# An attention and two mixtures in one kernel: the units of a head pair's round in another order, mask products as units of their own, the first mixture's early product in four pieces

## The chip, the cores and the metric

The kernel runs on one core of a Trainium2 chip. The metric is the time of one execution on the device in microseconds (us), as the median of repeated runs. The engines of the core work side by side, each in its own program order: TensorE (PE in the profile, its weight loads PEld), VectorE (DVE), ScalarE (ACT), GpSimd (POOL), and SyncE (SP), which here issues the DMAs. An engine waits for another by a semaphore, and then all that stands behind the waiting instruction on that engine waits too.

## The reference, cut to what matters

```python
def _attn_ref(q, k, v):                      # 4 batches, 8 heads, 576 tokens, 64 wide
    scores = scale * np.matmul(q, k.transpose(0, 1, 3, 2))
    scores = np.where(block_i >= block_j, scores, -1000000000.0)   # blocks of 64 tokens
    attn = np.exp(scores - np.max(scores, axis=-1, keepdims=True))
    attn = attn / (np.sum(attn, axis=-1, keepdims=True) + 1e-09)
    return np.matmul(attn, v)
...
def _moe_ref(x, w_in, w_out):                # x: 2304 x 512, w_in: 512 x 2048
    h = x @ w_in
    g = np.where(h >= 1, h, np.where(h <= -1, 0.0, (h + 1) ** 2 / 4))
    return g @ w_out
...
def _moe2_ref(x, phi, w1, w2):               # soft mixture: 8 experts, 4 slots each
    logits = x @ phi                         # softmax over tokens gives the slots' inputs,
    ...                                      # two products per expert, softmax over slots combines
```

The attention's output, turned to 2304 tokens by 512, is the first mixture's x, and that mixture's output is the second one's.

## The kernel before

The attention comes first and works on **pairs**: two heads of one batch, 16 pairs, one `Pair` object each. After it, `Moe.run` does the rest of the first mixture and the second. Only the attention's part of the program and a few early steps of the first mixture that are laid into it are touched.

What a pair needs is cut into small **units**, methods of `Pair` that each give one engine a few instructions. `lk`, `lq`, `lv` load keys, queries and values (SP). `kh`, `kl`, `qh`, `ql` split keys and queries into a high and a low part (ACT, POOL, ACT, DVE; `ql` also issues two small DMAs that lay out the last 64 queries, `QD`). `sc4` to `sc0` multiply scores (PE): three products of the parts; for `sc0` to `sc3` the two halves of a 64-row pair run on the two row halves of the array, and two small products with `low` and `one` then add the mask; `sc4` has no mask. `mx` takes the maxima (DVE), `ex` the exponentials with their sums (ACT), `rs` the reciprocal of the sums (DVE), `no` scales by it (POOL). `pt0` to `pt6` turn the scaled blocks, 25 of them, by products with the identity (PE), and `pc0` to `pc6` copy each group of up to four blocks out of PSUM (ACT, groups 1 and 3 DVE). `pa` and `pb` multiply by the values (PE) and `xh`, `xl` write the result out of PSUM as x (ACT and DVE, in high and low part for the first 1024 tokens, else one DVE copy). `w0`, `w1`, `w2` prepare a half of a 128-column strip of w_in (a load by SP; one ACT and four DVE instructions; three POOL ones, the last two of them sums of two arrays).

The order is written out by hand in the string `PLAN`. Each entry is a unit with a digit ahead of it; in round `it` it is done for pair `it - digit`. The entries' order is the program's order, in which each engine takes the units that are its own. Eleven **early units** of the first mixture (`EARLY`) go in from round 9 on, one a round: the entry `hm` is the product of one strip of w_in with 512 tokens (12 matmuls, each 512 columns, into one PSUM bank `h`), `ha` the first step of the bend (ACT) and `ho` the last two (DVE), after which the bank is free. The 64-row pair's scores have two PSUM tiles (`psc`), the values' product of `pa` has one (`ppv`), and all else, the groups `p0` to `p6`, the product `o` of `pb` and the early product `h`, takes turns in three banks (`ptr`): whoever takes a bank waits until its last content is copied out. The order in which the banks are given back in the program decides which one comes next.

From line 273 on, `attention` makes a list of (pair, unit) from `PLAN`, and calls the units one by one. The profile calls lines 120 and 123 the scores and their masks, 113 `sc4`, 166 the turning, 184 and 189 the values' product, 527 the early product, 142 and 140 the maxima, 147 the exponentials, 152 and 153 the reciprocal, 158 the scaling, 83 `kl`, 248 and 250 the copies, 545 `ha`, 558 and 559 `ho`.

Of the kernel before, what the change touches and what calls it, by code (L numbers as in the profile page):

```python
# [7 lines left out]
F32 = mybir.dt.float32  # L8
# [6 lines left out]
P = 128  # L15
# [21 lines left out]
class Pair:  # L37
# [69 lines left out]
    def sc(self, i):  # L107
        e, nc = self.e, self.nc
        sc = self.scs[i] = e.psc.tile([P, 2, 512], F32, tag="sc", name=f"sc{self.nm}{i}")
        if i == 4:  # L110
            for k, (qa, ka) in enumerate(((0, 0), (0, 1), (1, 0))):
                for u in range(2):
                    nc.tensor.matmul(sc[:, u, 0:288], self.QD[:, qa], self.K[:, ka, 288 * u:288 * u + 288],
                                     start=(k == 0), stop=(k == 2))
            return
        n = 128 * (i + 1)
        rows = slice(0, 64), slice(64, 128)
        for k, (qa, ka) in enumerate(((0, 0), (0, 1), (1, 0))):
            for h, r in enumerate(rows):
                nc.tensor.matmul(sc[:, h, 0:n], self.Q[r, qa, 128 * i:128 * i + 128], self.K[r, ka, 0:n],  # L120
                                 start=(k == 0), stop=False)
        for h, r in enumerate(rows):
            nc.tensor.matmul(sc[:, h, n - 64:n], e.low[r], e.one[r], start=False, stop=True)  # L123

    def block(self, i):
        for u, b in enumerate(self.TILES[i]):
# [18 lines left out]
    def ex(self, i):  # L145
        for b, sc, pr in self.block(i):
            self.nc.scalar.activation(pr, sc, AF.Exp, bias=self.negm[:, b:b + 1], accum_out=self.sums[:, b:b + 1])  # L147
# [66 lines left out]
    def xl(self, a):  # L214
        for hi, lo, src in self.xparts(a):
# [4 lines left out]


PLAN = """
3sc4 4pc2 4no1 1ho0 4pt4 3ex2 2qh 4pt5 4pc5 3sc1 4pc4 3rs0 3mx4 3mx1 5pa
3ex4 3ex1 2ql 5xh1 5pb 2w2 5xh0 3rs2 3no2 4pc3 3no3 5xl1 3sc0 2sc3
3pt0 3mx0 3no4 5xl0 3pt1 1kh 1lq 2mx3 3lv 3ex0 3rs1 3pc1 4pt6 2sc2 0hm0
2mx2 1w1 3pc0 4pc6 2ex3 0ha0 1kl 0lk 3pt2 3pt3 3no0 0w0
"""
EARLY = {(9, 0): (0, 0), (10, 0): (0, 1), (11, 0): (0, 2), (12, 0): (0, 3), (13, 0): (1, 0), (14, 0): (0, 4),
         (15, 0): (1, 1), (16, 0): (0, 5), (17, 0): (1, 2), (18, 0): (0, 6), (19, 0): (1, 3)}
# [12 lines left out]
def attention(e, tc, nb=4, wl=(1, 1 + 2 * READY)):  # L242
    nc = tc.nc
    e.ENG = ENG

    def copy(eng, dst, src):
        if eng == "A":
            nc.scalar.copy(dst, src)  # L248
        elif eng == "D":
            nc.vector.tensor_copy(dst, src)  # L250
        else:
            nc.gpsimd.tensor_scalar(out=dst, in0=src, scalar1=1.0, scalar2=1.0, op0=ALU.mult, op1=ALU.mult)
    e.copy = copy
    e.eng = lambda c: nc.vector if c == "D" else nc.gpsimd

    e.QD, e.pr, e.v_ = [], [], []
    for i in range(2):
        e.QD.append(e.apool.tile([P, 2, P], F32R, tag=f"QD{i}", bufs=1, name=f"QD{i}"))
        z = (nc.gpsimd, nc.vector)[i]
        z.memset(e.QD[i][0:64, :, 64:P].bitcast(F32), 0.0)  # L260
        z.memset(e.QD[i][64:P, :, 0:64].bitcast(F32), 0.0)
        e.pr.append([e.apool.tile([P, P * (b // 2 + 1)], F32, tag=f"pr{i}{b}", bufs=1, name=f"pr{i}{b}")
                     for b in range(9)])
        z.memset(e.pr[i][8][:, 576:640], 0.0)
        e.v_.append(e.apool.tile([P, 5, 2, 64], F32, tag=f"natv{i}", bufs=1, name=f"vn{i}"))
        z.memset(e.v_[i][64:P, 4], 0.0)
    e.low = e.apool.tile([P, P], mybir.dt.bfloat16, tag="low", bufs=1, name="low")
    e.one = e.apool.tile([P, 64], mybir.dt.bfloat16, tag="one", bufs=1, name="one")
    nc.vector.memset(e.low, 0.0)
    nc.vector.memset(e.one, 1.0)  # L270
    for h in (0, 64):
        nc.vector.memset(e.low[h:h + 1, 0:64], -2.0 ** 127)
    pairs = [Pair(e, nc, b, p) for b in range(nb) for p in range(4)]
    n = len(pairs)
    plan = [(it - int(u[0]), u[1:]) for it in range(n + 6) for u in PLAN.split()]
    plan = [(i, u) for i, u in plan if ((i, int(u[2:])) in EARLY if u[0] == "h" and u[1] in "moa" else
                                        0 <= i < n if u[0] != "w" else wl[0] <= i < wl[1])]
    fill = [(int(u[0]), u[1:]) for u in FILL.split()]
    assert sorted(fill) == sorted(plan[:len(fill)])
    for i, u in fill + plan[len(fill):]:  # L280
        if u[0] == "h":
            e.moe.early(u[1], *EARLY[i, int(u[2:])])
        elif u[0] != "w":
            pairs[i].step(u)
        else:
            t, c = (i - wl[0]) // 2, slice((i - wl[0]) % 2 * 256, (i - wl[0]) % 2 * 256 + 256)
            if u == "w0" and c.start == 0:
                e.moe.w_raw(t)
            elif u == "w1":
                e.moe.w_mul(t, c)  # L290
                e.moe.w_bits(t, c)
            elif u == "w2":
                e.moe.w_parts(t, c, e.ENG["w"])
# [14 lines left out]
class Moe:  # L308
# [207 lines left out]
            self.g[b, f] = self.new([P, a, n], F32, f"g{b}_{f}")  # L516
        return self.g[b, f // a * a][:, f % a]

    def h_unit(self, b, f, mid=()):
        e, nc = self.e, self.nc  # L520
        n = self.BLK[b][1]
        w = self.w[f].rearrange("p a (k c) -> p a k c", k=4)
        ph = self.ph[b, f] = e.ptr.tile([P, 512], F32, tag="tr", name=f"h{b}_{f}")
        m = 0
        for kk in range(4):
            for wi, xi in ((0, 0), (0, 1), (1, 0)):
                nc.tensor.matmul(ph[:, 0:n], w[:, wi, kk], self.x(b, kk, xi)[:, 0:n], start=(m == 0), stop=(m == 11))  # L527
                m += 1
            if kk == 2:
                for fn, *a in mid:  # L530
                    getattr(self, fn)(*a)
        if f == 15:
            self.drop_x(b)
        if b == 4:
            self.drop(f"w{f}")
# [23 lines left out]
        nc.vector.tensor_tensor(out=g, in0=ph, in1=g, op=ALU.max)  # L559

    def early(self, what, b, f):
        if what == "m":
            self.h_unit(b, f)
        elif what == "a":
            self.bend_act(b, f, "D")
        else:
            self.bend_max(b, f, "D")
# [547 lines left out]
def tile_attention_mixtures(ctx, tc, q, k, v, w_in, w_out, phi, w1, w2a, w2b, outa, outb):  # L1115
# [33 lines left out]
    with tc.tile_pool(name="att", bufs=1, reuse_waits="tile") as e.apool:  # L1149
        attention(e, tc)  # L1150
        nc.sync.dma_start(e.phi, phi.rearrange("(k p) s -> p k s", p=P))
# [53 lines left out]
```

## Time and profile before

| | |
|---|---|
| median of 3 runs | 538.68 us (538.38 to 539.71) |
| the profiled execution | 538.28 us, of which 536.5 us are the span from its first to its last instruction |
| busy share of the span | PE 95%, PEld 72%, DVE 64%, ACT 60%, POOL 38% |
| mean granted TensorE clock | 0.985 |
| first scores; first product of `Moe.run` | 5.6 us; 209 us |

A row of the trace's timeline has the start in us, the time in us from there to the last end of a group of equal instructions, the engine and line, the operation with its tiles (output, then inputs), the shape and the number of instructions. In brackets stands how long the engine sat idle just before, and what ended that. The starts of two groups give what the first of them cost its engine; a group's own time overlaps the next by the tail of the last product.

### The profile page before, as it was taken

The page shows a single profiled execution, that of the slowest core. Times are in us where ns is not written, and L with a number is a line of the kernel's source. Part 1 is how long each engine was busy: PE and PEld are TensorE (multiplying, and loading weights), DVE is VectorE, ACT ScalarE, POOL GpSimd, SP SyncE. Part 2 cuts the span into 40 slices and gives each one's busy share as a digit, 9 for nine tenths or more (in the row PEclk, how much of TensorE's full clock was granted, in tenths as well). Part 3 has the DMA queues.
Part 4 walks back from the last instruction along what each step waited for, and adds up shares of the span by engine and source line. Part 5 has one row for each costly group of instructions (what it writes and reads, how often), then busy time and mean ns, then how long its engine had stood idle before and what let it go on. Part 6 is the DMA issues. An engine that isn't in the chain of part 4 may idle for free.

```text
span 536.5 us, 11758 instructions
## 1 busy us (share of the span) xinstructions
PE 507.3 (95%) x4538; PEld 384.6 (72%) x4538; DVE 343.0 (64%) x676; ACT 322.4 (60%) x732; POOL 201.6 (38%) x259
## 2 busy tenths in 40 slices
PE   6899999999999989999989999899999999989994
PEld 5687777777777767878767887788767888643463
DVE  7799998888886734888998645823464343531242
ACT  5899987777777642667768878634334545231131
POOL 4888986767775430555552212500001000010000
PEclk9799999999999999999999999999999999999997
DMA  4444454323221135412146875322176496799997
GB/s 154 118 125 124 117 129 121 101 85 110 73 72 51 28 106 188 160 46 78 41 137 230 281 265 168 121 93 83 25 258 227 158 374 217 256 339 399 410 413 303
DMA packets 42711, 91.01 MB, mean 170 GB/s; under 512 B 8736, under 2 KB 18080, under 8 KB 42656
## 3 DMA queue, kind: packets, MB, share of 16 engines
q1 hardware_dynamic: 42656, 90.26, 49.6%
q8 instruction: 36, 0.59, 0.5%
q14 instruction: 19, 0.16, 0.1%
HBM read 74.51 MB, written 14.68 MB: 166 GB/s over the span
## 4 chain that ended last, share of the span: by engine, by line
PE 65%; DVE 14%; ACT 7%; DMA 5%; issue 3%; POOL 0%; SPq 0%; DVEq 0%; ACTq 0%; POOLq 0%
PE h L527 32%; PE gn L581 5%; PE om L184 4%; PE sc L120 4%; PE lt L593 3%; PE s L631 3%; PE eh L987 3%; DMA ew<-in_w2b_dram 3%; ACT pr L147 2%; DVE nm L142 2%; DVE wab L455 2%; DVE g L559 2%; DVE g L558 2%; ACT g L545 1%; PE om L189 1%
## 5 line engine op out<-in xcount | busy, mean ns | idle before, releaser
L527 PE MATMUL h<-xh,w 128*128 128x512 f32 (+1 forms) x384 | 115.6, 368 | 0.0
L158 POOL TENSOR_SCALAR pr<-pr,sm 128x384 f32<-128x384 f32 (+2 forms) x144 | 86.3, 617 | 38.4 <-DVE sm L153 14.0
L527 PE MATMUL h<-xt,w 128*128 128x512 f32 x384 | 91.6, 395 | 1.7 <-ACT PT L248 1.7
L558 DVE SCALAR_TENSOR_TENSOR g<-g 128x512 f32<-128x512 f32 (+1 forms) x52 | 37.4, 720 | 82.3 <-ACT g L545 81.7
L147 ACT ACTIVATE pr<-sc,nm 128x512 f32<-128x512 f32 (+2 forms) x144 | 78.6, 559 | 11.9 <-DVE nm L142 8.6
L527 PEld LDWEIGHTS h<-xt,w 128*128 128x128 f32 x384 | 70.5, 188 | 18.6 <-ACT PT L248 2.1
L527 PEld LDWEIGHTS h<-xh,w 128*128 128x128 f32 x384 | 69.1, 189 | 13.7 <-issue 3.8
L545 ACT ACTIVATE g<-h,half 128x512 f32<-128x512 f32 (+1 forms) x52 | 32.4, 623 | 62.5 <-PE h L527 62.0
L527 PE MATMUL h<-xl,w 128*128 128x512 f32 (+1 forms) x192 | 68.2, 355 | 0.2 <-POOL xl L400 0.2
L559 DVE TENSOR_TENSOR g<-h,g 128x512 f32<-128x512 f32 (+1 forms) x80 | 50.8, 636 | 16.0 <-ACT g L550 14.0
L142 DVE TENSOR_REDUCE nm<-sc 128x2 f32<-128x1024 f32 (+1 forms) x64 | 51.8, 818 | 5.0 <-PE sc L123 4.4
L662 POOL TENSOR_TENSOR cn<-cn,cm 128x128 f32<-128x128 f32 (+1 forms) x5 | 1.9, 378 | 140.7 <-DVE cm L661 111.2
L120 PE MATMUL sc<-K,Q 64*128 64x512 f32 (+3 forms) x384 | 47.0, 360 | 3.6 <-ACT pr L147 3.2
L248 ACT COPY gn<-gn 128x1024 f32<-128x1024 f32 x35 | 35.3, 1009 | 16.0 <-PE gn L581 15.8
L527 PEld LDWEIGHTS h<-xl,w 128*128 128x128 f32 x192 | 36.4, 189 | 4.5 <-POOL xl L400 0.7
L120 PEld LDWEIGHTS sc<-K,Q 64*128 64x128 f32 x384 | 29.9, 194 | 13.3 <-ACT pr L147 6.7
L472 POOL TENSOR_TENSOR wab<-wab,w 128x256 f32<-128x256 f32 (+1 forms) x23 | 22.5, 980 | 40.9 <-ACT w L248 20.4
L465 POOL TENSOR_TENSOR wab<-wab 128x512 f32<-128x512 f32 x16 | 21.9, 1372 | 40.4 <-DVE wab L457 27.3
L581 PE MATMUL gn<-ident,g 128*128 128x128 f32 x280 | 36.5, 273 | 0.2 <-ACT gn L248 0.2
L581 PEld LDWEIGHTS gn<-ident,g 128*128 128x128 f32 x280 | 31.9, 140 | 5.4 <-issue 2.5
L455 DVE SCALAR_TENSOR_TENSOR wab<-wab 128x512 uint32<-128x512 uint32 (+1 forms) x39 | 28.5, 731 | 9.8 <-ACT wab L448 6.9
L547 ACT ACTIVATE g<-h,half 128x512 f32<-128x512 f32 x28 | 19.3, 688 | 22.5 <-PE h L527 20.1
(221 smaller groups left out, 901.7 us busy)
## 6 DMA issues: line engine op xcount, KB each, us to landing
ew<-in_w_dram SPq DMA_DIRECT2D x32, 512.0 KB, 6.3
raw<-in_w_in_dram SPq DMA_DIRECT2D x16, 512.0 KB, 5.3
raw<-in_w_out_dram SPq DMA_DIRECT2D x16, 512.0 KB, 4.1
ew<-in_w2a_dram SPq DMA_DIRECT2D x16, 510.0 KB, 8.8
ew<-in_w2b_dram SPq DMA_DIRECT2D x16, 344.0 KB, 6.8
kn<-in_k_dram SPq DMA_DIRECT2D x16, 288.0 KB, 3.9
qn<-in_q_dram SPq DMA_DIRECT2D x16, 288.0 KB, 3.2
vn<-in_v_dram SPq DMA_DIRECT2D x16, 256.0 KB, 3.3
```

The costliest lines, as they stand in the source:

```text
L120: nc.tensor.matmul(sc[:, h, 0:n], self.Q[r, qa, 128 * i:128 * i + 128], self.K[r, ka, 0:n], start=(k == 0), stop=False)
L142: nc.vector.tensor_reduce(out=self.negm[:, 2 * i:2 * i + 2], in_=self.scs[i][:, :, 0:128 * (i + 1)], axis=AX.X, op=ALU.max, negate=True)
L147: self.nc.scalar.activation(pr, sc, AF.Exp, bias=self.negm[:, b:b + 1], accum_out=self.sums[:, b:b + 1])
L158: self.nc.gpsimd.tensor_scalar(out=pr, in0=pr, scalar1=self.sums[:, b:b + 1], scalar2=1.0, op0=ALU.mult, op1=ALU.mult)
L248: nc.scalar.copy(dst, src)
L455: v.scalar_tensor_tensor(out=Au, in0=Au, scalar=3, in1=Bu, op0=ALU.logical_shift_left, op1=ALU.bitwise_or)
L472: p.tensor_tensor(out=A, in0=A, in1=w[:, 0].bitcast(F32), op=ALU.subtract)
L527: nc.tensor.matmul(ph[:, 0:n], w[:, wi, kk], self.x(b, kk, xi)[:, 0:n], start=(m == 0), stop=(m == 11))
L545: nc.scalar.activation(g, ph, AF.Relu, bias=e.half[:, 0:1], scale=0.5)
L558: nc.vector.scalar_tensor_tensor(out=g, in0=g, scalar=1.0, in1=g, op0=ALU.min, op1=ALU.mult)
L559: nc.vector.tensor_tensor(out=g, in0=ph, in1=g, op=ALU.max)
L581: nc.tensor.transpose(ps[:, j, i * P:(i + 1) * P], self.gt(b, f)[:, o:o + P], e.ident)
```

## The change

Three things change. The mask's two products leave `sc` and are the unit `mk`, with entries of their own in the plan. The early product is cut into four units of three matmuls, `hm`, `hx`, `hy` and `hz`, by the four 128-row slices of x; the bank is taken at `hm`. And `PLAN` has all its entries in another order, with other digits: a round begins elsewhere, and some units are done a round later for their pair.

```diff
-        for h, r in enumerate(rows):
-            nc.tensor.matmul(sc[:, h, n - 64:n], e.low[r], e.one[r], start=False, stop=True)
+
+    def mk(self, i):
+        n = 128 * (i + 1)
+        for h, r in enumerate((slice(0, 64), slice(64, 128))):
+            self.nc.tensor.matmul(self.scs[i][:, h, n - 64:n], self.e.low[r], self.e.one[r], start=False, stop=True)
...
 PLAN = """
-3sc4 4pc2 4no1 1ho0 4pt4 3ex2 2qh 4pt5 4pc5 3sc1 4pc4 3rs0 3mx4 3mx1 5pa
...
+4pt1 4pc0 3mx3 4rs1 4no4 3sc2 4lv 3mk2 5pc6 4pc1 0w0 2kl 6xh1 5pt5 1hm0
+0lk 3mx2 4no1 4pt3 6xl1 3ex3 5pc5 4pt2 4pc3 3sc4 4no0 1hx0 3mx4 1hy0 2qh
...
-    plan = [(i, u) for i, u in plan if ((i, int(u[2:])) in EARLY if u[0] == "h" and u[1] in "moa" else
+    plan = [(i, u) for i, u in plan if ((i, int(u[2:])) in EARLY if u[0] == "h" and u[1] in "mxyzoa" else
...
+    def h_part(self, b, f, kk):
+        e, nc = self.e, self.nc
+        n = self.BLK[b][1]
+        if kk == 0:
+            self.ph[b, f] = e.ptr.tile([P, 512], F32, tag="tr", name=f"h{b}_{f}")
+        ph, w = self.ph[b, f], self.w[f].rearrange("p a (k c) -> p a k c", k=4)
+        for m, (wi, xi) in enumerate(((0, 0), (0, 1), (1, 0))):
+            nc.tensor.matmul(ph[:, 0:n], w[:, wi, kk], self.x(b, kk, xi)[:, 0:n], start=(kk + m == 0), stop=(kk + m == 5))
+
...
         for kk in range(4):
-            for wi, xi in ((0, 0), (0, 1), (1, 0)):
-                nc.tensor.matmul(ph[:, 0:n], w[:, wi, kk], self.x(b, kk, xi)[:, 0:n], start=(m == 0), stop=(m == 11))
-                m += 1
+            self.h_part(b, f, kk)
...
     def early(self, what, b, f):
-        if what == "m":
-            self.h_unit(b, f)
+        if what in "mxyz":
+            self.h_part(b, f, "mxyz".index(what))
```

On every engine the instructions are the same in number and kind; only their order differs. Names below: `h0_2` is the early product of batch of tokens 0 with strip 2, `ps2_0p2` group `p2` of batch 2, pair 0, `sc2_14` the scores `sc4` of batch 2, pair 1.

TensorE in a round with an early product, before: the twelve matmuls of `h` stand together, behind them `p2`, `p3`, `sc4` and then `p4` and `p5` of one pair.

```order
L527 MATMUL h0_2_1691<-xt00_140,w2_918 128x512 x3
L527 MATMUL h0_2_1691<-xt01_141,w2_918 128x512 x3
L527 MATMUL h0_2_1691<-xt02_142,w2_918 128x512 x3
L527 MATMUL h0_2_1691<-xt03_143,w2_918 128x512 x3
L166 MATMUL ps2_0p2_1719<-ident_116,pr08_176 128x128
...
L166 MATMUL ps2_0p3_1724<-ident_116,pr05_173 128x128
...
L113 MATMUL sc2_14_1733<-K_2_1_1482,QD1_180 128x288 x6
L166 MATMUL ps2_0p4_1745<-ident_116,pr00_168 128x128
...
L166 MATMUL ps2_0p5_1754<-ident_116,pr08_176 128x128
```

The same place now:

```order
L169 MATMUL ps1_3p5_1689<-ident_116,pr18_191 128x128
...
L530 MATMUL h0_2_1694<-xt00_140,w2_1040 128x512 x3
L169 MATMUL ps2_0p3_1703<-ident_116,pr05_173 128x128
...
L169 MATMUL ps2_0p2_1712<-ident_116,pr08_176 128x128
...
L113 MATMUL sc2_14_1718<-K_2_1_1460,QD1_180 128x288 x6
L530 MATMUL h0_2_1694<-xt01_141,w2_1040 128x512 x3
L530 MATMUL h0_2_1694<-xt02_142,w2_1040 128x512 x3
L530 MATMUL h0_2_1694<-xt03_143,w2_1040 128x512 x3
L169 MATMUL ps2_0p4_1744<-ident_116,pr00_168 128x128
...
L187 MATMUL ps1_3o_1750<-PT1_3_1481,vn1_193 64x256 x2
```

`p5` is now turned one round later and stands ahead of `h`; three of `h`'s matmuls come ahead of `p3`, `p2` and `sc4`, nine behind them, and the part `o` of the values' product follows `p4` ahead of `sc1`, where before it followed `pa`.

ScalarE at the same place, before: the bend of `h` (`g`) stands between the exponentials of `sc3` and the copy of `p2`.

```order
L147 ACTIVATE pr17_190,sm2_1_1670<-sc2_13_1643,nm2_1_1669 128x512
L545 ACTIVATE g0_2_1714<-h0_2_1691,half_129 128x512
L248 COPY PT2_0_1678<-ps2_0p2_1719 128x512
L147 ACTIVATE pr14_187,sm2_1_1670<-sc2_12_1682,nm2_1_1669 128x384
L147 ACTIVATE pr15_188,sm2_1_1670<-sc2_12_1682,nm2_1_1669 128x384
L89 ACTIVATE Q_2_2_1752<-qn2_2_1667 128x576
L248 COPY PT2_0_1678<-ps2_0p5_1754 128x512
```

And now:

```order
L150 ACTIVATE pr17_190,sm2_1_1668<-sc2_13_1634,nm2_1_1667 128x512
L252 COPY PT1_3_1481<-ps1_3p5_1689 128x512
L89 ACTIVATE Q_2_2_1734<-qn2_2_1392 128x576
L150 ACTIVATE pr14_187,sm2_1_1668<-sc2_12_1673,nm2_1_1667 128x384
L150 ACTIVATE pr15_188,sm2_1_1668<-sc2_12_1673,nm2_1_1667 128x384
L252 COPY PT2_0_1665<-ps2_0p2_1712 128x512
L150 ACTIVATE pr18_191,sm2_1_1668<-sc2_14_1718,nm2_1_1667 128x576
L551 ACTIVATE g0_2_1773<-h0_2_1694,half_129 128x512
```

The bend of `h` has moved behind the exponentials of `sc2` and `sc4`, and the copy of `p5`, whose bank `p2` takes, stands behind the exponentials of `sc3`.

## Rows read from the trace of the kernel before

**Rows 1.** Busy time by stretch: us, each engine's busy time, clock, DMA.

```profile
9.93:69.59 59.66, 55.64 (x546) 44.44 (x546) 53.88 (x116) 53.58 (x165) 51.66 (x77) 0.91 0.44 123
69.59:185.06 115.47, 112.65 (x1072) 89.61 (x1072) 92.84 (x202) 85.65 (x249) 78.86 (x115) 1.00 0.30 84
```

**Rows 2.** Timeline of TensorE: sc4 of the first pair and of the seventh.

```profile
9.93 1.03 PE L113 MATMUL sc<-K,QD 128*128 128x288 f32 x6 [2.66 <-DVE wab L456]
...
69.59 1.06 PE L113 MATMUL sc<-K,QD 128*128 128x288 f32 x6 [0.24 <-ACT pr L147]
```

**Rows 3.** Timeline of TensorE in one round with an early product.

```profile
133.29 1.03 PE L166 MATMUL ps_2p<-ident,pr 128*128 128x128 f32 x8
134.08 1.05 PE L113 MATMUL sc<-K,QD 128*128 128x288 f32 x6
134.97 1.37 PE L166 MATMUL ps_2p<-ident,pr 128*128 128x128 f32 x8
136.27 0.62 PE L120 MATMUL sc<-K,Q 64*128 64x256 f32 x6
136.74 0.21 PE L123 MATMUL sc<-one,low 64*128 64x64 bf16 x2
136.87 1.74 PE L184 MATMUL om<-PT,vn 128*64 128x256 f32 x16
...
139.77 0.55 PE L120 MATMUL sc<-K,Q 64*128 64x128 f32 x6
140.16 0.20 PE L123 MATMUL sc<-one,low 64*128 64x64 bf16 x2
140.20 0.94 PE L120 MATMUL sc<-K,Q 64*128 64x512 f32 x6
...
142.38 0.79 PE L120 MATMUL sc<-K,Q 64*128 64x384 f32 x6
...
143.18 3.06 PE L527 MATMUL h<-xt,w 128*128 128x512 f32 x12
146.08 1.03 PE L166 MATMUL ps_3p<-ident,pr 128*128 128x128 f32 x8
```

**Rows 4.** Timeline of TensorE: four turnings behind sc4, two rounds earlier.

```profile
110.38 0.66 PE L166 MATMUL ps_0p<-ident,pr 128*128 128x128 f32 x4 [0.70 <-DVE g L559]
```

**Rows 5.** Timelines of VectorE and ScalarE: one maximum, one exponential, one copy.

```profile
46.55 1.22 DVE L142 TENSOR_REDUCE nm<-sc 128x2 f32<-128x1024 f32 x1
...
117.07 0.58 ACT L248 COPY PT<-ps_1p 128x512 f32<-128x512 f32 x1
...
117.70 0.72 ACT L147 ACTIVATE pr<-sc,nm 128x512 f32<-128x512 f32 x1
```

**Rows 6.** Timeline of TensorE at the end of the attention.

```profile
185.06 1.04 PE L113 MATMUL sc<-K,QD 128*128 128x288 f32 x6
...
191.27 1.09 PE L166 MATMUL ps_3p<-ident,pr 128*128 128x128 f32 x8
...
193.83 3.02 PE L527 MATMUL h<-xt,w 128*128 128x512 f32 x12 [1.32 <-ACT PT L248]
...
209.09 4.15 PE L527 MATMUL h<-xt,w 128*128 128x512 f32 x17
```

**Rows 7.** Timelines of GpSimd (kl) and VectorE (reciprocals' first step), rounds without early product.

```profile
44.40 0.15 DVE L152 TENSOR_SCALAR sm<-sm 128x1 f32<-128x1 f32 x1
...
47.68 0.65 DVE L152 TENSOR_SCALAR sm<-sm 128x4 f32<-128x4 f32 x1
...
46.88 1.42 POOL L83 TENSOR_TENSOR K<-kn,K 128x576 fp32r<-128x576 f32 x1
```

**Rows 8.** Timeline of ScalarE at the start: second pair's keys, first strip's weights.

```profile
6.61 0.67 ACT L248 CAST K<-kn 128x576 fp32r<-128x576 f32 x1 [1.48 <-DMA kn<-in_k_dram]
...
8.06 0.43 ACT L448 ACTIVATE wab<-raw 128x256 f32<-128x256 f32 x1 [0.79 <-DMA raw<-in_w_in_dram]
```

**Rows 9.** Chain that ended last, near the end: start, us, what.

```profile
501.95 8.59 DMA ew<-in_w2b_dram
```

More of the change, by code (lines that the diff above doesn't have):

```diff
@@ L222 @@
 PLAN = """
-3sc4 4pc2 4no1 1ho0 4pt4 3ex2 2qh 4pt5 4pc5 3sc1 4pc4 3rs0 3mx4 3mx1 5pa
-3ex4 3ex1 2ql 5xh1 5pb 2w2 5xh0 3rs2 3no2 4pc3 3no3 5xl1 3sc0 2sc3
-3pt0 3mx0 3no4 5xl0 3pt1 1kh 1lq 2mx3 3lv 3ex0 3rs1 3pc1 4pt6 2sc2 0hm0
-2mx2 1w1 3pc0 4pc6 2ex3 0ha0 1kl 0lk 3pt2 3pt3 3no0 0w0
+4pt1 4pc0 3mx3 4rs1 4no4 3sc2 4lv 3mk2 5pc6 4pc1 0w0 2kl 6xh1 5pt5 1hm0
+0lk 3mx2 4no1 4pt3 6xl1 3ex3 5pc5 4pt2 4pc3 3sc4 4no0 1hx0 3mx4 1hy0 2qh
+2ql 3ex2 1hz0 4pt4 4pc2 5pb 3w2 0lq 3sc1 3ex4 3mk1 3rs0 1ha0 1ho0 5xh0
+4pc4 3no2 3mx1 5pa 2w1 3ex1 3sc0 3mk0 2sc3 5xl0 2mk3 1kh 3mx0 3rs2 3ex0
+4pt6 3no3 3pt0
 """
@@ L517, in gt, with h_unit @@
         return self.g[b, f // a * a][:, f % a]
-    def h_unit(self, b, f, mid=()):
+    def h_part(self, b, f, kk):
         e, nc = self.e, self.nc
         n = self.BLK[b][1]
-        w = self.w[f].rearrange("p a (k c) -> p a k c", k=4)
-        ph = self.ph[b, f] = e.ptr.tile([P, 512], F32, tag="tr", name=f"h{b}_{f}")
-        m = 0
+        if kk == 0:
[3 more added lines that the diff above has]
+            nc.tensor.matmul(ph[:, 0:n], w[:, wi, kk], self.x(b, kk, xi)[:, 0:n], start=(kk + m == 0), stop=(kk + m == 5))
+    def h_unit(self, b, f, mid=()):
         for kk in range(4):
-            for wi, xi in ((0, 0), (0, 1), (1, 0)):
-                nc.tensor.matmul(ph[:, 0:n], w[:, wi, kk], self.x(b, kk, xi)[:, 0:n], start=(m == 0), stop=(m == 11))
-                m += 1
+            self.h_part(b, f, kk)
             if kk == 2:
```

## The prediction

> **What bounds the kernel now.** I read the busy table of the page first, then the busy time by stretch, the chain of waits, and the timelines of the engines in single rounds. PE is busy 95% of the span, so nearly everything that a new order can give back is small waits of PE, and the change touches only the attention, the first 209 us. That part has three stretches. From `sc4` of the first pair to `sc4` of the seventh (9.93 to 69.59 us, [rows 2]) there are six rounds without an early product, 59.66 / 6 = 9.94 us each; VectorE, ScalarE and GpSimd are all busy for 52 to 54 of those 59.66 us, PE for 55.64 [rows 1]: nobody has room, and in the chain of waits the work of VectorE and ScalarE alternates. From there to `sc4` of the last pair come nine rounds with one, 115.47 / 9 = 12.83 us each; PE is busy 112.65 of 115.47 us, VectorE 92.84 [rows 1]: here PE is the bound. Then the pipeline drains, 185.06 to 209.09 us [rows 6].
>
> In a PE-bound round the question is what PE waits for. Eight turnings that follow `h` take 134.08 - 133.29 = 0.79 us; the eight behind `sc4` (`p4`, `p5`) take 136.27 - 134.97 = 1.30 us [rows 3]. The row that shows the reason stands two rounds earlier: the second four start late, and DVE L559 ended the wait [rows 4]. That is `ho`: `p5` takes the bank that `h` holds until the bend is done. So each round loses 0.51 us there, and more in the rounds where the row itself says 0.70.
>
> **The change part by part.** *Mask units.* `mk` stands on PE right behind its `sc` as before, since what was put between are units of SP, ACT and DVE. It costs and gives nothing; PE's order there is the same.
>
> *The round with an early product.* `p5` moves away from `h`'s bank: now it takes the bank that `p0`'s copy gives back, and the next user of `h`'s bank is `p0` of the next pair, at the round's end. The 0.51 us go. What is late next? `p2` now takes the bank of `p5`, whose copy on ACT stands behind the exponentials of `sc3`. Count from the start of `p1`: the masks of `sc3` ended some 0.5 us earlier (five turnings at 0.10). Its maximum takes 1.22, the two exponentials 2 x 0.72 less overlap, about 1.34, the copy 0.58 less overlap, about 0.5 [rows 5]: ready at about -0.5 + 1.15 + 1.35 + 0.5 = 2.5. PE reaches `p2` after `p1` 0.4, `sc2` with mask 143.18 - 142.38 = 0.8, `p5` 0.4, a quarter of `h` (146.08 - 143.18 = 2.90) 0.7 and `p3` 0.4, that is 2.7. The cover is thin, 0.2 us; if it goes, each tenth of a microsecond costs 9 x 0.1.
>
> The new order also splits groups. `pb` stands ahead of `sc1` and `pa` behind it, so the array changes its shape once more a round (64-row halves, full, 64-column halves: seven changes for six). A mask that is followed by the same shape costs 140.20 - 140.16 = 0.04 us, one that is followed by another shape 136.87 - 136.74 = 0.13 [rows 3]: +0.09 us. `p5` and `p4` stand alone now, each between 0 and 0.66 - 0.40 = 0.26 us dearer [rows 4]; PE does not wait there, so I take them at nothing. Sum: 12.83 - 0.51 + 0.09 = 12.4 us, bounds 12.2 (the rounds with the longer wait gain more) and 12.83 (the wait only moves).
>
> The Trainium skill, "TensorEngine Tiling (Array Packing)", Key Properties, says that changing the tiling mode drains TensorE, which speaks against splitting `pa` and `pb`. The trace agrees in kind, with 0.09 us a change. By the page alone, without a size, only a loss would follow; by the row it is the +0.09 above.
>
> *The end.* From `sc4` of the last pair to the end of its `sc0` was 191.27 - 185.06 = 6.21 us [rows 6]. Now three quarters of `h` stand in it: 0.89 (`sc4`) + 2.18 + 0.40 (`p4`) + 0.60 (`sc1`) + 2.90 (`pa`, `pb`) + 0.43 (`sc0`) = 7.40 us [rows 3]; in exchange the nine rounds between the `sc4`s hold 2.18 us less. Behind it stood 209.09 - 191.27 = 17.82 us; PE's work there was 26 turnings at 0.10, two `h` and two `pa` with `pb` at 2.90 each, 14.2 us, so 3.6 us were waits, 1.32 of them for ACT's copy behind the last exponentials [rows 6]. Now 30 turnings are left, 14.6 us. The copy of `p0` behind the last exponentials still comes late: it was done 193.83 - 191.27 = 2.5 us after `sc0`, and is done some 0.9 earlier, since VectorE takes the maximum at once. PE has 0.9 us of turnings until it needs it, so 0.7 us of wait, and I add 0.4 for small ones: 15.7 us, bounds 14.6 and 16.9. The other early product covers the rest.
>
> So from 69.59 us to the attention's end: 9 x 12.4 - 2.18 + 7.40 + 15.7 = 132.5 us, where it was 139.5: **-7.0** us, bounds 9 x 12.2 - 2.18 + 7.40 + 14.6 = 129.6 (-9.9) and 9 x 12.83 - 2.18 + 7.40 + 16.9 = 137.6 (-1.9).
>
> *The rounds without one.* PE is not the bound, so its waits are worth less. What the order changes is who collides. The first step of the reciprocal takes 0.15 us in one place and 0.65 in another; the 0.65 ends at 48.33, where `kl` on GpSimd, 46.88 + 1.42, ends at 48.30 [rows 7]: VectorE is held until GpSimd's two-array operation is over, 0.5 us. Now `kl` stands behind `no4` and meets `rs1` about a third earlier in it: up to 1.42 us held, +0.92. The copy of `p1` and then `p2` hang behind. The lower end is that the 0.5 goes and PE's 55.64 / 6 = 9.27 is reached, -0.67. I take +0.15, near nothing, since the other collisions (`w2`'s sums, now ahead of `rs0`) can go either way: 6 x 0.15 = **+0.9** us, bounds -4.0 and +5.5.
>
> *The start.* SP issues the first strip of w_in ahead of the second pair's keys. The keys came at 6.61 us and the strip at 8.06 [rows 8]; exchanged, the copy of the keys (0.67) rather than the strip's step (0.43) delays the first exponentials: **+0.2** us, bounds -1.0 (VectorE's four strip instructions, which stood ahead of the third maximum, come later) and +1.4.
>
> *Behind the attention* nothing is reordered. The last products of pair 15, on which the first strips of `Moe.run` hang, come at the same distance from the end. So the gain carries over.
>
> Sum: -7.0 + 0.9 + 0.2 = -5.9 us. Against the profiled execution, 538.28, that is 532.4; the median of the runs shown is 0.4 higher, which I leave out.
>
> **The rivals.** *The wait only moves* (B): `p2` waits for `p5`'s copy, as long as `p5` waited before. For it speaks the cover of 0.2 us; against it that VectorE has 22 us free in this stretch [rows 1], so that the maximum seldom starts late. The rounds stay at 12.83: -7.0 + 9 x 0.43 = -3.1, with the other terms -2.0, 536.3 us.
>
> *Held by GpSimd* (C), the one that ends slower: in the six rounds `rs1` is held for all of `kl`, 1.42, and `rs0` for the two sums of `w2`, about as long, 2.84 us in place of about 1.0; everything on VectorE stands behind. 6 x 1.84 = 11.0, so -7.0 + 11.0 + 0.2 = +4.2, 542.5 us. It decides from (7.0 + 1.6) / 6 = 1.4 us a round on. Against it: a round has idle time on VectorE of 9.94 - 53.88 / 6 = 0.96 us, and a late `rs0` delays only GpSimd's scaling, which is needed at the round's end. The Trainium skill, "SBUF — State Buffer", section "SBUF: two separate sides", says that the ports which VectorE and GpSimd share are locked for a whole instruction and that the loser fully blocks. The trace agrees (48.33 and 48.30); by that rule alone C would be the likely case, but the rule does not say who starts first.
>
> *The gain is lost behind the attention* (D): near the end the chain waits 8.59 us for weights [rows 9]. If those loads came at their own pace, an earlier attention would only wait longer: 538.3 us. Against it: they are issued from the 31st unit of `Moe.run` on, into buffers that PE frees, so they move with it.
>
> *More than that* (E): the collisions vanish too, -9.9 - 2: about 527 us.
>
> **How the numbers follow.** Forecast 0.60; B 0.15; D, and partial C, 0.11; C 0.09; E 0.05. Changes within 0.3% (1.6 us) can't be told from none here. Faster: the forecast, E and most of B, 0.78; same: D and the rest of B, 0.13; slower: C, 0.09. The range reaches from between E and the forecast, 528.5, to B and D, 538.5; outside are C and most of E.
>
> **What would show it.** Right: `sc4` to `sc4` 12.3 to 12.5 us in the rounds with an early product, no row in which turnings wait for DVE's last bend step, the drain about 23 us from the last `sc4` to the first product of `Moe.run`, and the rest of the program as long as before. Wrong: a wait of `p2` for ACT (B), a reciprocal's first step of 1 us and more and rounds of over 10.5 us ahead of the seventh pair (C), a longer stretch behind the attention (D).

## The result

The changed kernel takes **541.96 us** (median of 7 runs, 540.23 to 542.52), the kernel before 538.68 (537.74 to 539.71): the ratio is 1.0055, with a 95% interval of 1.0037 to 1.0072. The change costs 0.55% of the time where 1.1% of gain was forecast, and 541.96 us lies above the range. The profiled execution has a span of 540.3 us (before 536.5).

The busy time by stretch, cut at the same places as in [rows 1] (`sc4` of the first, seventh and last pair, first product of `Moe.run`); the columns are stretch and length, then busy us of PE, its weight loads, VectorE, ScalarE, GpSimd, the clock, the DMA share, GB/s:

```profile
10.34:76.63 66.29, 57.63 (x545) 45.09 (x546) 62.67 (x117) 54.01 (x165) 48.16 (x75) 0.91 0.41 121
76.63:188.62 111.99, 110.51 (x1065) 87.24 (x1064) 100.98 (x205) 87.10 (x249) 76.18 (x118) 1.00 0.27 75
188.62:212.04 23.42, 22.72 (x224) 18.13 (x222) 10.79 (x25) 9.71 (x26) 5.28 (x9) 1.00 0.33 106
```

Set against [rows 1, 2, 6] they give the whole difference of the spans:

| stretch | before us | after us | measured | predicted |
|---|---|---|---|---|
| up to the first `sc4` | 9.93 | 10.34 | +0.41 | +0.2 |
| six rounds without an early product | 59.66 | 66.29 | **+6.63** | +0.9 |
| nine rounds with one | 115.47 | 111.99 | **-3.48** | -6.05 |
| last `sc4` to the end of the attention | 24.03 | 23.42 | -0.61 | -0.93 |
| behind the attention | 327.41 | 328.26 | +0.85 | 0 |
| sum | 536.5 | 540.3 | +3.8 | -5.9 |

The sign was lost in one place: the six rounds without an early product went from 9.94 to 11.05 us each, and VectorE's busy time in them from 53.88 to 62.67 us, for 116 and 117 instructions. The last of these rounds by itself, before and then after (columns as above), shows that VectorE has become the bound, busy for 10.97 of 11.25 us:

```profile
59.64:69.59 9.95, 9.71 (x108) 7.74 (x108) 9.60 (x22) 9.53 (x30) 9.02 (x14) 1.00 0.53 154
65.38:76.63 11.25, 10.04 (x110) 7.76 (x109) 10.97 (x22) 9.55 (x30) 8.29 (x14) 1.00 0.41 128
```

An instruction is called held here when it lasts longer than in other places while an operation of the other engine runs beside it. The timeline of VectorE and GpSimd at the end of a round of the changed kernel (start, us, engine, line, what) shows one that is:

```profile
61.73 1.20 DVE L145 TENSOR_REDUCE nm<-sc 128x2 f32<-128x1024 f32 x1
62.85 1.28 DVE L155 TENSOR_SCALAR sm<-sm 128x4 f32<-128x4 f32 x1
64.16 0.18 DVE L156 RECIPROCAL sm<-sm 128x4 f32<-128x4 f32 x1
64.26 0.66 DVE L254 COPY PT<-ps_0p 128x512 f32<-128x512 f32 x1
...
61.98 0.74 POOL L161 TENSOR_SCALAR pr<-pr,sm 128x576 f32<-128x576 f32 x1 [1.36 <-DVE sm L156]
62.69 1.41 POOL L83 TENSOR_TENSOR K<-kn,K 128x576 fp32r<-128x576 f32 x1
```

`rs1` (L155) adds a constant to 4 numbers per partition. It takes 0.15 us where nothing holds it (the 0.15 in [rows 7] is `rs2` with one number; the kernel with `kl` moved, below, has `rs1` itself at 0.16) and took 0.65 in its place before [rows 7]; now it begins 0.16 us after `kl` and ends, at 64.13, 0.03 us after `kl`'s end at 64.10. Behind it stand `p1`'s copy and then TensorE's `p2`, as TensorE's timeline there shows:

```profile
63.72 0.60 PE L169 MATMUL ps_0p<-ident,pr 128*128 128x128 f32 x4
64.97 0.66 PE L169 MATMUL ps_0p<-ident,pr 128*128 128x128 f32 x4 [0.66 <-DVE PT L254]
```

The groups of VectorE's instructions in these six rounds (busy us, mean ns of one) show which others were stretched: first the kernel before, then the changed one. L455 to L457, then L459 to L461, are the last three of the four bit operations of `w1`.

```profile
L152 DVE TENSOR_SCALAR sm<-sm 128x4 f32<-128x4 f32 (+1 forms) x18 | 8.0, 442 | 0.6 <-ACT pr L147 0.6
L95 DVE SCALAR_TENSOR_TENSOR Q<-qn,Q 128x576 fp32r<-128x576 f32 x6 | 4.7, 787 | 0.0
L457 DVE SCALAR_TENSOR_TENSOR wab<-raw,wab 128x256 f32<-128x256 uint32 x6 | 3.0, 498 | 0.2
L455 DVE SCALAR_TENSOR_TENSOR wab<-wab 128x256 uint32<-128x256 uint32 x5 | 2.1, 427 | 0.5
L456 DVE TENSOR_SCALAR wab<-wab 128x256 uint32<-128x256 uint32 x5 | 1.5, 294 | 0.2
```

```profile
L155 DVE TENSOR_SCALAR sm<-sm 128x4 f32<-128x4 f32 (+1 forms) x18 | 10.5, 584 | 0.0
L95 DVE SCALAR_TENSOR_TENSOR Q<-qn,Q 128x576 fp32r<-128x576 f32 x6 | 6.1, 1022 | 0.0
L461 DVE SCALAR_TENSOR_TENSOR wab<-raw,wab 128x256 f32<-128x256 uint32 x6 | 4.7, 789 | 0.2
L143 DVE TENSOR_REDUCE nm<-sc 128x1 f32<-128x576 f32 x6 | 4.5, 749 | 3.4 <-PE sc L113 3.3
L460 DVE TENSOR_SCALAR wab<-wab 128x256 uint32<-128x256 uint32 x6 | 4.0, 672 | 0.2
L459 DVE SCALAR_TENSOR_TENSOR wab<-wab 128x256 uint32<-128x256 uint32 x6 | 3.7, 614 | 0.6
```

The reciprocals' additions cost 2.5 us more and the query's split `ql` 1.4 more (it meets the sums of `w2`). The largest part is the bit operations of `w1`: these three take 0.86 us more a round by their means, some 5 us in six rounds, since they now stand beside GpSimd's scaling; before, GpSimd sat idle until the second of them was done (0.76 us in one round). So more than `rs1` is held, and the experiments have to tell which hold costs time. A held instruction is shown as a long one, not as a wait: VectorE looks busy.

In the rounds with an early product the aimed-at wait is gone: no turning waits for the bend any more, as one did in [rows 4]. TensorE's timeline behind the first piece of `h`, in a round early in the stretch and in a later one:

```profile
111.83 0.95 PE L530 MATMUL h<-xt,w 128*128 128x512 f32 x3
112.96 1.09 PE L169 MATMUL ps_0p<-ident,pr 128*128 128x128 f32 x8 [0.18 <-DVE PT L254]
...
162.16 0.95 PE L530 MATMUL h<-xt,w 128*128 128x512 f32 x3
162.99 1.09 PE L169 MATMUL ps_0p<-ident,pr 128*128 128x128 f32 x8
```

From the first product to the turnings `p3`, `p2` it is 1.13 us in the one and 0.83 in the other. Three rounds took 12.72 to 12.74 us, the five after them 12.34 to 12.44, and the one ahead of them, which holds a quarter of an early product only, 11.70.

### The profile page after: what moved, and what is told of

It is laid out like the page before. It is cut to its first block, busy times and chain, and to the rows that moved or that the text cites. A ratio compares the mean times of both kernels' runs of the same rounds, so it can differ in the third digit from the quotient of the medians.

```text
span 540.3 us, 11720 instructions
## 1 busy us (share of the span) xinstructions
PE 508.8 (94%) x4538; PEld 384.7 (71%) x4538; DVE 358.8 (66%) x676; ACT 324.4 (60%) x732; POOL 195.5 (36%) x259
## 4 chain that ended last, share of the span: by engine, by line
PE 64%; DVE 18%; DMA 7%; ACT 5%; issue 3%; POOL 1%; SPq 0%; DVEq 0%; ACTq 0%; POOLq 0%
PE h L530 32%; PE gn L587 5%; DVE nm L145 4%; DMA ew<-in_w2b_dram 4%; PE lt L599 3%; PE sc L120 3%; PE s L637 3%; PE eh L993 3%; PE om L187 2%; DVE sm L155 2%; DVE wab L459 2%; DMA kn<-in_k_dram 2%; PE sc L113 2%; DVE wab L460 2%; DVE wab L461 1%
## 5 line engine op out<-in xcount | busy, mean ns | idle before, releaser
L161 POOL TENSOR_SCALAR pr<-pr,sm 128x384 f32<-128x384 f32 (+2 forms) x144 | 83.5, 596 | 57.8 <-DVE sm L156 54.1
L530 PE MATMUL h<-xt,w 128*128 128x512 f32 x384 | 93.1, 395 | 0.0
L564 DVE SCALAR_TENSOR_TENSOR g<-g 128x512 f32<-128x512 f32 (+1 forms) x52 | 36.2, 696 | 80.2 <-ACT g L551 79.6
L459 DVE SCALAR_TENSOR_TENSOR wab<-wab 128x512 uint32<-128x512 uint32 (+1 forms) x39 | 29.8, 764 | 9.8 <-ACT wab L452 6.8
```

The source lines that it names most:

```text
L161: self.nc.gpsimd.tensor_scalar(out=pr, in0=pr, scalar1=self.sums[:, b:b + 1], scalar2=1.0, op0=ALU.mult, op1=ALU.mult)
L459: v.scalar_tensor_tensor(out=Au, in0=Au, scalar=3, in1=Bu, op0=ALU.logical_shift_left, op1=ALU.bitwise_or)
L564: nc.vector.scalar_tensor_tensor(out=g, in0=g, scalar=1.0, in1=g, op0=ALU.min, op1=ALU.mult)
```

## The experiments

Theory H: in the new order GpSimd's operations hold VectorE where VectorE is the bound. Rival O: VectorE is late because of the order of its own units, and what is held only fills idle time. Ratios are to the kernel before, with 95% intervals.

**`kl` moved away from `rs1`**

```diff
 0w0
-2kl
 6xh1
...
 4no0
+2kl
 1hx0
```

> The changed kernel with one unit moved: kl (GpSimd's subtraction of two arrays, 1.41 us) stands behind no0 instead of behind lv, so that rs1 on VectorE no longer begins while it runs. Theory H: rs1 goes from 1.28 to 0.15 us in every round; p3 and p2 no longer wait for p1's copy, so the first five rounds with h go from 12.74 to 12.44 (-1.5 us), and the rounds without h lose 0.4 to 1.1 us each (less where kl, or the sums of w2 pushed behind it, hold another VectorE instruction such as ql, 0.75 us free), -2.4 to -6.6 us: 534 to 538 us. Rival O: rs1 gets shorter, VectorE waits elsewhere, 541 to 543 us.

Measured: 538.17 us, ratio 0.9996 (0.9979 to 1.0014): the kernel's loss is gone, just short of H's 534 to 538. The six rounds take 62.43 us (10.26 to 10.28 each in the last three), 3.86 less than in the changed kernel and still 2.8 more than before; VectorE is busy 56.28 us in them. Its timeline, and GpSimd's:

```profile
54.84 0.78 DVE L95 SCALAR_TENSOR_TENSOR Q<-qn,Q 128x576 fp32r<-128x576 f32 x1
55.54 0.70 DVE L155 TENSOR_SCALAR sm<-sm 128x4 f32<-128x4 f32 x1
...
61.34 0.16 DVE L155 TENSOR_SCALAR sm<-sm 128x4 f32<-128x4 f32 x1
...
55.10 1.12 POOL L475 TENSOR_TENSOR wab<-wab,w 128x256 f32<-128x256 f32 x1
```

`rs1` takes 0.16 again (-1.12 against the changed kernel), `ql` 0.78 (-0.47), the four bit operations 2.08 in place of 2.52 (-0.44), and `rs0` is now held instead, 0.70 (+0.55): -1.48 on VectorE, of which 0.51 comes back as waits, and the round is 0.98 shorter. So the move freed more than `rs1`. Holding works the other way too: GpSimd's sum begins inside `ql` and takes 1.12 us where the next takes 0.73. The second half of the expectation failed. I had counted five rounds of 12.74 us, there are three, and they did not move. TensorE and ScalarE in one of them:

```profile
108.15 0.94 PE L529 MATMUL h<-xt,w 128*128 128x512 f32 x3
108.93 1.39 PE L169 MATMUL ps_0p<-ident,pr 128*128 128x128 f32 x8
...
107.43 0.35 ACT L215 CAST xt<-om 128x192 fp32r<-128x192 f32 x1
...
108.98 0.63 ACT L251 COPY PT<-ps_3p 128x512 f32<-128x512 f32 x1
```

The eight turnings take 1.15 us to the next group instead of some 0.8: with `p3` free, `p2` waits for `p5`'s copy (108.98), which stands on ScalarE behind two exponentials and a split of `x` (L215) that the later rounds do not have. That is rival B of the prediction, in three rounds.

**The bit operations moved away from the scaling**

```diff
 3mk1
+2w1
 3rs0
...
 5pa
-2w1
 3ex1
```

> The changed kernel with one unit moved: w1 (a multiply on ScalarE and four bit operations on VectorE) stands ahead of rs0 instead of behind the first mixture's PV product pa, so that VectorE does it while GpSimd idles, and not beside GpSimd's scaling no2 and no3. Theory H (GpSimd's two-ended use holds VectorE, which is the bound of the rounds without h): the four bit operations go back from 0.43 + 0.62 + 0.68 + 0.79 = 2.5 us to about 1.7 us a round, the rounds without h from 11.05-11.25 to about 10.4 us, six of them 4.8 us, so about 537 us. Rival O (VectorE is late because of the order of its own units, and what is held only fills time in which it would wait): the bit operations get shorter, VectorE waits instead, 541 to 543 us.

Measured: 546.37 us, ratio 1.0146 (1.0121 to 1.0171): slower still, beyond O's 541 to 543 too, though the four operations took 1.43 us a round instead of 2.52. Timelines of one round:

```profile
53.91 1.23 DVE L145 TENSOR_REDUCE nm<-sc 128x2 f32<-128x1024 f32 x1 [1.24 <-PE sc L126]
55.05 0.93 DVE L155 TENSOR_SCALAR sm<-sm 128x4 f32<-128x4 f32 x1
...
52.86 0.96 PE L120 MATMUL sc<-K,Q 64*128 64x512 f32 x6 [1.09 <-ACT pr L150]
...
51.79 0.47 ACT L150 ACTIVATE pr<-sc,nm 128x256 f32<-128x256 f32 x1 [1.40 <-DVE nm L145]
```

`w1` now stands ahead of `mx1`; ScalarE waits 1.40 us for that maximum, TensorE 1.09 for ScalarE to free the score bank, VectorE 1.24 for TensorE's scores. The rounds stay at 11.2 us, and the first two grow to 12.96 and 11.95. Here O was right in kind: the time that was freed came back as a wait, in a loop through three engines. So the summed busy time of VectorE is not the price; what counts is a delay with something due behind it. What the held bit operations cost where they are is not settled by this run.

**The addition left out**

```diff
-        nc.vector.tensor_scalar(out=s, in0=s, scalar1=1e-9, scalar2=None, op0=ALU.add)
         nc.vector.reciprocal(s, s)
```

> The changed kernel without the addition of 1e-9 to the softmax sums (the TENSOR_SCALAR of rs; every sum holds exp(0) = 1, to which 1e-9 adds nothing in f32), so that the reciprocal alone is left of rs. GpSimd's work, kl among it, stays where it is. Theory F (VectorE is held by the form of its instruction: the addition was held 1.28 us beside kl, a reciprocal, 0.18 us in every place so far, is not): rs1 no longer waits for kl, the rounds without h go from 11.2 to about 10.1 us, where TensorE's 9.75 to 10.0 us of work is near (six times -1.1), and the first five with h from 12.74 to 12.44 (-1.5): 534 us. Theory G (whatever stands there waits until kl is done): the reciprocal takes about 1.3 us there, 541 us.

> The kernel before without the addition of 1e-9, the base for the two others: rs0 and rs1 are held there too (0.69 and 0.65 us), but its rounds without h take 9.7 to 10.1 us with TensorE busy 9.7 of it, and in its rounds with h VectorE is not the bound. Theory: at most 0.2 us a round in six rounds, 537.5 to 538.5 us. If VectorE's held time were the price in every order, 1.2 us a round in six rounds: 531 us.

> The kernel of e6_klhx without the addition of 1e-9. There rs0 is still held (0.70 us) by GpSimd's sums of w2, and the rounds without h take 10.28 us with VectorE busy nearly all of it. Theory F: 0.70 + 0.16 + 0.14 us less on VectorE in each round, the rounds without h near TensorE's 9.75 to 10.0 us of work, six times -0.3, the rest as in e6_klhx: 534.5 us. Theory G: reciprocal held instead, 536 us.

Measured, without the addition: the changed kernel 535.92 us, ratio 0.9956 (0.9940 to 0.9971); the kernel before 536.54, 0.9971 (0.9957 to 0.9984). The timelines of the first:

```profile
53.34 0.75 DVE L95 SCALAR_TENSOR_TENSOR Q<-qn,Q 128x576 fp32r<-128x576 f32 x1
...
59.73 0.17 DVE L155 RECIPROCAL sm<-sm 128x4 f32<-128x4 f32 x1
...
59.57 1.42 POOL L83 TENSOR_TENSOR K<-kn,K 128x576 fp32r<-128x576 f32 x1
```

The reciprocal runs inside `kl` in its usual 0.17 us. With GpSimd's order untouched, the six rounds fall from 66.29 to 61.34 us. This is the cleanest evidence for H, as far as the additions go: the loss of the changed kernel goes with the form of one instruction of 4 elements that met `kl`. (The two other additions that went took 0.15 and 0.14 us and were not held.) It is not `rs1` alone that changed: `ql` is no longer held either (0.75 for 1.25), and the bit operations take 2.14 us for 2.52. In the kernel without the addition and with `kl` and `hx` moved, below, `ql` (1.15) and the bit operations (2.35) are held and `rs1` is not: its rounds take 10.53 us, against 11.28 with `rs1` held and `hx` moved. So most of the difference goes with `rs1`; the price of the other holds is not shown singly. The Trainium skill, "SBUF — State Buffer", section "SBUF: two separate sides", names as the VectorE instructions that need the shared ports those in a two-port mode or with two SBUF inputs; the rows agree that the lock depends on the form (addition 1.28, reciprocal 0.17 beside the same `kl`).

The rounds came to 10.33 us rather than the 10.1 expected, with VectorE now waiting for `sc4`, `sc1` and ScalarE, and the three slow rounds with an early product to 12.58, not 12.44. The same edit is worth 1.0% in the new order (from 1.0055 to 0.9956) and 0.3% in the old one, where `rs0` and `rs1` took 0.69 and 0.65 us in each of the six rounds. Held time was almost free in these: they take 59.58 us without the addition and 59.66 with it. The kernel came out below the 537.5 to 538.5 expected, and where its 0.3% arises is not shown: in the two traces the six rounds, the nine and the end each differ by 0.2 us or less.

**Pieces of `h` next to each other**

`hx` beside `hm`, so that six products cover the bank of `p3` and `p2`; the second kernel has `kl` moved as well, the third has all four pieces where `hz` stood.

```diff
 1hm0
+1hx0
 0lk
...
-1hx0
 3mx4
```

> The changed kernel with hx next to hm, kl left where it is. If the first five rounds with h take 12.74 instead of 12.44 us only because TensorE reaches p3 and p2 before their banks are free (whatever holds VectorE), six products ahead of them are cover enough: those rounds 12.44, -1.5 us: 540.4 us, with the rounds without h at 11.05 to 11.25 as before. If VectorE itself is their bound (it goes round from rs1 to rs1 in 12.74 us, 1.28 of it held), nothing changes: 542 us.

> The changed kernel with kl behind no0 (as in e2_kl) and with h's second piece hx next to its first, so that six products of h stand ahead of the turnings p3 and p2 and six behind sc4. In e2_kl the first five rounds with h still took 12.74 us though rs1 was free: p2 had to wait for ScalarE's copy of p5, which stands behind two exponentials and, in those rounds, a split of x. Theory P (that wait for a bank is what is left): the three products cover it, those rounds go to 12.44, -1.5 us against e2_kl: 536.7 us. Rival (with only six products behind sc4, p4 now waits for p3's copy and what it had covered comes back): 538 us or more.

> The changed kernel with h's four pieces in one place, where hz stands (behind sc4 and the second mixture's query split), the rest of its order kept: what the spreading of h alone brings. Theory: without hm ahead of p3 and p2 these two wait for their banks another 0.5 to 0.8 us in each of ten rounds, 547 to 550 us. Rival (the pieces are only for show, TensorE does the same work in any order): 542 us.

Measured: `hx` moved 540.62 us, ratio 1.0052 (1.0033 to 1.0071); the nine rounds 111.07 us for 111.99, the three slow ones 12.38 to 12.49, as forecast for want of cover, though the ratio can't be told from the changed kernel's 1.0055. With `kl` moved too, **536.33 us, ratio 0.9967 (0.9951 to 0.9984)**, faster than both kernels: six rounds 63.50, nine rounds 110.49. All pieces in one place: 545.30 us, ratio 1.0132 (1.0107 to 1.0157), rounds of 12.85: slower, by less than the 547 to 550 expected. TensorE's timelines of the second and then the third:

```profile
107.95 1.63 PE L529 MATMUL h<-xt,w 128*128 128x512 f32 x6
109.42 1.03 PE L169 MATMUL ps_0p<-ident,pr 128*128 128x128 f32 x8
```

```profile
113.95 0.60 PE L169 MATMUL ps_0p<-ident,pr 128*128 128x128 f32 x4
114.87 0.66 PE L169 MATMUL ps_0p<-ident,pr 128*128 128x128 f32 x4 [0.32 <-DVE PT L253]
```

With six products ahead the turnings follow each other at 0.10 us; with none they stop for a bank, and the round is as long as before the change (12.85 against 12.83). So the 0.4 us a round that the change does gain hangs on pieces of `h` standing in front of the turnings; three products are enough cover in the later rounds, six in all. Leaving out the addition in the second of these kernels too gave 535.14 us, 0.9947 (0.9930 to 0.9965). The six rounds took 61.92 us for 63.50, near the forecast of -1.8, but not in the way forecast: the first three together got shorter and the last three longer (10.53 us after 10.28):

```profile
53.26 1.15 DVE L95 SCALAR_TENSOR_TENSOR Q<-qn,Q 128x576 fp32r<-128x576 f32 x1
...
55.96 0.58 DVE L457 SCALAR_TENSOR_TENSOR wab<-wab 128x256 uint32<-128x256 uint32 x1 [0.63 <-ACT wab L450]
```

`ql` is held again and the bit operations wait for ScalarE; the freed time shifted who meets whom.

**Parts of the change, and the two orders in one kernel**

> The order of the kernel before, but with the mask products as units right behind their score products and h in its four pieces one after the other: the parts of the change without the new order. Theory: the parts alone cost and bring nothing, 538.7 us within 1. Rival: a unit of its own costs TensorE something (0.15 us a round by 16 rounds), 541 us.

```diff
 3sc1
+3mk1
...
 0hm0
+0hx0
+0hy0
+0hz0
```

Measured: 537.38 us, ratio 0.9992 (0.9976 to 1.0009). The parts alone do nothing; it is the order.

> The kernel before with two units moved: p5's turning and its copy stand behind the score product sc1 instead of ahead of it, and nothing else of the change. Theory S (what the new order can win in the rounds with h is the 0.51 us for which TensorE's turning p5 waits for h's bank): sc1 now covers VectorE's last bend step, the rounds with h go from 12.75 to about 12.35, nine of them -3.6 us, the others stay: 535 us. Rival (the wait only moves: p5 comes 0.8 us later, so its copy on ScalarE and the exponentials behind it, and TensorE waits for a score bank instead): 538 to 539 us.

```diff
-4pt5
-4pc5
 3sc1
+4pt5
+4pc5
 4pc4
```

Measured: 541.69 us, ratio 1.0063 (1.0041 to 1.0085): the rival, and worse than its 538 to 539. Timelines:

```profile
112.88 0.62 PE L120 MATMUL sc<-K,Q 64*128 64x256 f32 x6 [0.28 <-ACT pr L147]
...
113.48 0.66 PE L166 MATMUL ps_0p<-ident,pr 128*128 128x128 f32 x4
...
117.13 0.29 DVE L210 COPY xw<-om 128x128 f32<-128x128 f32 x1 [1.89 <-ACT xt L212]
```

`p5` no longer waits for `h`'s bank, and TensorE does `p4`, `sc1` and `p5` in 2.06 us instead of 2.49. But ScalarE's copies come later; VectorE waits 1.89 us for ScalarE's split of `x` (1.08 at the same place before). The mean round with `h`, from the second to the last, is 12.98 us against 12.83, and the six rounds without take 62.12 against 59.66. A wait of 0.51 us can be removed on the engine that is the bound and win nothing.

> Both orders in one kernel: pairs 1 to 6 by the order of before (whose rounds without h take 9.94 us), pairs 7 to 16 by the order of after. Theory H: the two effects are local to their rounds and add up, so the loss of 6.6 us in the first six rounds goes and the gain of the rounds with h and of the end stays: 535 us within 1.5. Rival: the crossing from one order to the other costs over 2 us, or the gain of the later rounds hung on what the early ones left: 538 us or more.

```diff
-    plan = [(it - int(u[0]), u[1:]) for it in range(n + 6) for u in PLAN.split()]
+    plan = []
+    for which, text in enumerate((PLAN0, PLAN)):
+        us = text.split()
+        for it in range(n + 7):
+            for k, u in enumerate(us):
+                if (it - int(u[0]) >= SPLIT) == bool(which):
+                    plan.append((it + k / len(us) - which * SHIFT, which, it - int(u[0]), u[1:]))
+    plan = [(i, u) for _, _, i, u in sorted(plan, key=lambda x: x[:2])]
```

(`PLAN0` is the order of the parts kernel above, SPLIT 6, SHIFT 0.381, which lays the `sc4` of both orders on each other.) Measured: 542.30 us, ratio 1.0073 (1.0052 to 1.0094): the rival. The first five rounds took 50.1 us, like before (49.7), and from the ninth `sc4` on 12.36 to 12.75, like after; but the three rounds of the crossing took 14.27, 13.03 and 14.14 us, where before 9.95 stood for the first and after 11.70 and 12.74 for the other two: 7.05 us. The timelines in the first of them:

```profile
67.51 1.50 DVE L474 SCALAR_TENSOR_TENSOR wab<-raw,wab 128x256 f32<-128x256 uint32 x1
...
69.67 0.66 PE L169 MATMUL ps_1p<-ident,pr 128*128 128x128 f32 x4 [1.84 <-DVE PT L260]
```

A bit operation that takes 0.42 us with GpSimd idle takes 1.50 beside `kl`, and TensorE waits 1.84 us for the copy behind it. An order mixed without looking at who meets whom costs more than either.

## Why the prediction was wrong

*Rounds without an early product: this step failed.* The term was 0.15 us a round, near nothing, on the ground that the other collisions can go either way; it measured 1.1, beyond the +0.92 that I had taken for `rs1`'s upper end. The mechanism had been read rightly from [rows 7], down to 1.42 us of `kl` against 1.28 found. `rs1` itself grew by 0.63; the other collisions did not go either way but added to it (`ql` 0.24 and the bit operations some 0.9 us a round of VectorE's time). One mistake was to give a hold that the order makes nearly certain (released together by `rs2`, GpSimd does `no4`, 0.74 us, and VectorE `mx3`, 1.20, so that `rs1` must begin in the first half of `kl`) the value between its bounds. The other was to take VectorE's mean of 0.96 us of idle time in a round for cover. That mean hides where the idle time was: 4.2 of its 5.8 us lay in the first two rounds, and the last four had 0.35 to 0.48 us each (9.95 - 9.60 in the last of them); TensorE was busy 9.71 us in that one, so the lower end of 9.27 was out of reach too. In the changed kernel VectorE's one wait of note in the six rounds is 3.3 us, ahead of the first `mx4`; no cover was left for a hold on the path `mx3`, `rs1`, `p1`'s copy, `p2`.

*Rival C* was right in one of its two halves: `rs1` was held for nearly all of `kl` (1.28 us), but `rs0` was not held at all (0.15), since `ql` met the sums of `w2` in its place, and the bit operations were not in it. That its 542.5 us lies so near the 541.96 is in part luck: it had 1.84 us a round where 1.1 came, and a gain of 7.0 us in the later rounds and the end where 4.1 came. (E's sum, -11.9, gives 526.4 and not 527; nothing hangs on that.)

*Rounds with an early product: right in mechanism, too large in sum.* The forecast of 12.4 us is met from the eleventh `sc4` on (12.34 to 12.44). Taking the wait for `h`'s bank away would not have been enough: with `p5` moved alone nothing was gained, and without the quarter of `h` in front, 0.7 us in the prediction's count of the cover, the round stayed at 12.85. Two things were missed. In three rounds the thin cover of 0.2 us in front of `p2` was not there (12.73 us, so 1.0 us in all, and six products restore it). And the 2.18 us of `h` that leave the first round of this stretch could not all come off it: with a quarter of `h` it is nearly a round without one (VectorE busy for 11.42 of its 11.70 us). 12.4 - 2.18 = 10.2 us was expected, 11.70 came: 1.5 us.

*The end* was right: 23.42 us against 23.1, with `p0`'s copy awaited for 0.70 us as computed:

```profile
198.17 0.66 PE L169 MATMUL ps_2p<-ident,pr 128*128 128x128 f32 x4 [0.70 <-ACT PT L252]
```

*Mask units* at nothing: right, by the parts kernel. *The start*: +0.41 against +0.2, one trace each; what delayed it was not looked into. *Behind the attention* 0.85 us were added, against rival D, which asked for a gain that is lost there. No kernel here changes that part, and it took 326.4 to 328.8 us in the thirteen traces, so 0.85 us is within its scatter; where it arises there was not looked into.

## What to carry to other kernels

Before moving a unit on an engine that shares ports with another, list for both engines which instruction will run beside which, and charge the whole overlap where a held form meets a long operation on a path with no slack; a long bar for a 4-element instruction is a wait in disguise. A freed wait is worth something only if the next releaser on each engine comes early too: follow the loop through all of them (the maximum, the exponential, the bank), as the two single moves that removed a wait or a hold and lost time show. Read idle time round by round, since a mean over a stretch can put it where there is none. Pieces of independent matrix work in front of an operation that needs a bank back are good cover, and how many pieces it takes is a thing to measure.

## What the runs showed of the hardware

Which VectorE forms are held beside a GpSimd operation: the addition of a constant in SBUF (0.15 to 1.28 us), the two-array `ql` (0.75 to 1.26) and the bit operations (0.29 to 0.68 and 0.42 to 0.79 beside GpSimd's scaling by one factor, 0.42 to 1.50 beside `kl`; 0.28 to 0.43 with GpSimd idle); not held in any row shown: the maximum over PSUM (1.20), the copies out of PSUM (0.66), the reciprocal in SBUF (0.17). GpSimd in turn is held by VectorE (0.73 to 1.12). An addition and a reciprocal over the same 4 numbers differ in this.
